# A new order string for visits and jobs in a fused attention and feed-forward kernel

## The chip, the cores and the metric

The kernel runs on one core of one Trainium2 chip. The metric is device time in microseconds, from the start to the end of one execution; a comparison goes by the median of several executions.

## What is computed

One input `x` of 2048 rows and 640 columns is normalised row by row. Attention with 32 query heads of width 20 and a single key and value head shared by all of them, and a feed-forward block with a SiLU between its two matrices, both read the normalised rows, and their results are added to `x`. All arrays are bfloat16. Cut to what matters:

```python
x = A_x                                   # (1, 2048, 640)
xn = layernorm(x)
q = (xn @ wq) -> 32 heads of 20;  k = xn @ wk;  v = xn @ wv      # one k, v head
p = softmax(q @ k.T / sqrt(20));  o = p @ v;  A = concat(o) @ wo
B = silu(xn @ w1) @ w2                    # 640 -> 1728 -> 640
out = x + A + B
```

## The kernel before

The program is written by a planner. Python code creates every operation with its engine, an assumed duration and the keys that it reads and writes; a list scheduler runs a clock over five engines (`pe`, `act`, `dve`, `pool`, `sp`) and fixes the order of the operations on each of them; `emit` then writes each engine's list out, with a semaphore wait wherever an operation depends on another engine. So the order of work on the chip is fixed when the program is built, and the engines then run freely against each other's semaphores.

The scores are cut into blocks: 128 keys by 512 queries of one head. There are 32 heads x 4 query chunks x 16 key tiles = 2048 blocks, ordered in groups of 64 (four heads of one chunk). On PE the work after the prologue falls into three kinds of steps:

- A *visit* (`do_S`, matmuls at line 1133) computes the scores of one to four blocks, each into a PSUM bank of its own. Seven of the eight banks serve visits and jobs. Of a visit's blocks some go to ACT, which takes the exponential of up to three neighbouring banks with one instruction (line 1156, into tile `E`); where the free banks don't lie side by side, the exponential is split into several instructions. The others go to DVE, which builds an exponential from integer arithmetic: line 1173 converts and clamps the block into `Z`, and when three such blocks are together (or the group ends) `flush_z` makes two shifted copies of them, called Y. The second copy is always made by POOL (line 1207), the first by DVE (line 1201) or POOL (line 1207).
- A *P step* (`do_pv`, line 1047) multiplies four blocks of exponentials, one for each head of the group, with the values, in four column strips of the array at once. It accumulates in the eighth bank, which DVE copies out at the group's end (line 1251); a DMA transposes that, and DVE and POOL normalise it.
- A *J step* is one accumulation step of a job: a part of the query projection (`qd_job`), the first feed-forward matrix (`h_job`, 512 columns; its tanh on ACT is line 1395, its product on DVE line 1403) or the output (`out_job`, 320 columns). All of these are four matmuls at line 533 side by side, except the paired step at line 1385. Jobs come in a fixed order from a queue.

The order of the steps on PE is a string, `ORDER`, followed by `follow` from block 70 to the last: P is a P step, J a J step, and every other letter a visit. `VISITS` says what a letter means: its blocks, and how many of them go to DVE. The letter's case is handed on as `y0_on`: a capital sends the first Y copy to DVE, a small letter to POOL, if this visit happens to complete a set.

```python
VISITS = {"a": (3, 0), "b": (3, 1), "c": (3, 2), "e": (4, 1), "f": (4, 2), "g": (2, 0), "h": (2, 1),
          "k": (1, 0), "m": (1, 1), "d": (4, 3)}
```

When a step's inputs or banks aren't there yet by the planner's clock, the planner lets PE wait, or puts a short multiplication by zeros (`fill`, lines 954 and 967) in between. If a P step can't be taken, another may be taken early when a visit needs room, and the string then skips one. Which banks a visit gets, the places in `E`, and the order of the lists of ACT, DVE, POOL and SP all follow from the planner's clock as it goes along the string. After the string's end a tail finishes the last group and the output.

Of the kernel before, what the change touches and what calls it, by code (L numbers as in the profile page):

```python
# [79 lines left out]
YIELD = 0.65  # L80
VISITS = {"a": (3, 0), "b": (3, 1), "c": (3, 2), "e": (4, 1), "f": (4, 2), "g": (2, 0), "h": (2, 1), "k": (1, 0), "m": (1, 1), "d": (4, 3)}
ORDER = (
    "hhPbhPPPhHPbPPPfAPPPPCPBPPbPPFPPgHPPPhBJPJBJPcJJPhGPPPAJJPJCJJPbGPPPHhJPJHhJhhPgJPHhJGPHPGPPPFPPBPPb"
    "PmbPJJaJPcJJPPEPPPPHHHAPPMCPPgPPfJgJJJJGPbJJPPHhJHgPJJhgJPPPBJJbPPbJPBJPBPPPPFPPPAPPfPPJJbJJJPbbPPJJ"
    "JbJJbPPPFPPbJJJbJPJPEJJJJJPPeJJJJJPbhJJJJJPePPPPbPPfPPJJJBhPPJJPEJJJJPJHBJJJPJJPbGJJPPJPfPJPJbJJPPbJ"
    "PJbPJBJJJJbJJJbJPJbJJJbJJPbPPFPPPBPPFPPBPJJJbJJPJBPBJPJJbPJJJbJPJbPPfPPbPPPePJPJbJJBPJbJPJJbPJBJJJJB"
    "JJPbJJJJbPPFPPBPPbPPPEJJJJJJJBPPbJJJBJJJPbJPbPPPfPPbPPBPPePJJJbJPJBPPBJJPbJJJBJPJbJJJJbJJJbPPePPPPFP"
    "PBPPFPPAJJJJJJBPJJJBPJJbJJJbPPEPPPhhPPPfPPBJJJbJJBJJJPaJJbJPJJJPJbJJJbPJPbPPFPPBPPPePPPPFPPbPJPJPgFJ"
    "JJJJJJbJPbPPJbJJJbPPfPPPbPePJJJbJJPBJJBJPJJFPGPPPPbPPfPPJJJBHJJJJJJJePPPPPbcJJJJJBHJJJJJPePPPPbPPfPP"
    "PbJJbJJJbPJJPbJJJBPPbJJJJJBJhJJJJPePPPPBPPfPPBJJJJJbbPPPPPFPPbJJbJJBJPbJJJBJJbPPPPEPPPBPPJJfJJJPJJGb"  # L90
    "PJJJPfPPBPPBJJbPJJJPbBPPPPPBJJJJBJJJbJJJJbJJJJbJJJJbPFPPPPBfPPPPfPPbPPAPJbJJJPeJPPPbPPFPPBJJJJJBJJBJ"
    "JPJbJJPbPJJbJJJBJJPPBPEPPPPPFPPbPJPJbJJPbJJPbJJPbJJJBPPbJJJJBJJPBPPbJJPBPPPEPPbPPJJfJJGPJPFPPBPPBJJJ"
    "JbJJJbJJJJbJJJBJPJbJPJBPPbJPPbPPePPbJJPJJJEJPJJJJJHbPJPBJJPJBJJbPPJJbPPfPPBPPPePPPPFPPbPPJBJJbJJbPPP"
    "FPPBPJJJBJJBJJJJJJJeJPJJJJbJJPBPPEPPPPPdGPPPbPPbJPPBJJJbJJPBJJPBPPbJJJJbJJPBPJbJJJJbPPfPPBPPePJJJJJb"
    "JJJBJJJbJJJPbPJBPPPBJJJJbPPEPPPPFPPbPPPbPPfPPbJJJJJbbPPPJJJbJJbJJJJJPbPPbJPPbJJBJJbPPJJBJJJbPPPPfPPB"
    "PJJCJJJPePPPPaPPBJJJPfJJPPPbhJJJJJPFJJJJJPeJJJJJPBbPPPPJbJPbJJbPJBPPPFPPbPPbJJbJJJBPJJJbJJbJJJPBJJPB"
    "PPFPPBJJJJJBbPPPJJPbJJJbPPPbPPPBPPEPJJJbJJbPPPfPPBPPBJJJJBJJPbPJbJJPBJJJJBJJJJBPPbPJJbPPFPPAPPPfPPJJ"
    "JbJJJBJPJBJJJJbJJJbJJJJBPPePPBJPJJEJJPPBPPbPPPfPPbPPPFPPbPPBPPEPJJJJJBJPJJBJJJBJJJJBJJJJbPPfPPbPPPeP"
    "JJJJJbJJPBJJJBJJPBPPBJPJBJJJJBJPPbPPfPPPBPPePPPPFPPbJPJBJPbJJbPPPfPPBJJJJbJJPJJJJfGJJJJJJPJbJJPbPPfP"
    "PBPPPFPPbPPbPJJBJPJBJJPBPJJBJJJBJPJBPPBJJPBJPJbJPJBPPBPPEJJPJJJbJJPJbJPJBJPbJJJJBJPJbJJPBPPFPPbPPBPP"  # L100
    "PeJPJJJJbJJJBJPJbJJPBJJJbJJJJbPPBPPfPPPbPPePPJJBJJJPEPJJJhJJPePPPPPBPFPPJJbJJPJBPbPJJJcJJPHgJJPJJJGf"
    "PPPPPPbPPfPPBJJPBJPJJbHJJJJJEJJPJJJhbJJJJJPbPPPPePCPJJJJJbbPPPPPPfPPBJJJbPJbPJbJPJJCJJPBPGJJJJJPfGPP"
    "PPPBJJPBJJJJBJJPBJJJbJPPbPJBJJJPbJJJbPPfPPPBPPEPJJJJJbJJJbJJJJBJJJBJJJJbPPFPPAPPPfPPPPFPPBJJJPBJJJJB"
    "JJPaJJJJJJBJJJJPbPEPPPPfPPPPfPPBPPbPPFPPBJJJJBJJJBJPJJbPJJBJPbJPPbJPJBJJJBPPePJJPJJbJJPBPJJbJJJbJPJB"
    "PJJBJJPbJPJBPPFPPgPPEPPPPFPPPbPPFPPBJJJJbJJJBPJJbPJJPBbPJPJJeJJJPJJBPPfPPBPPFPPAPBPJJJJJJfJJJJJGbJJP"
    "JPeJJPJJPJfPbPPPFPPBPPePPbPJJJJEJJPPJJbJJPBJJJBPJbJPbJPJbPJJbPPBPPFPPBPPbPbPFPPbPBPPBPPFPbPPAPPPfbPb"
    "PPFaPPFPPbPPbPePPBPPPKbPJJJJJJBPJJBPPPePA"
)
Z_COST = 0.2
U_PRIO = 1.022  # L110
# [1891 lines left out]
```

## Time and profile before

| | |
|---|---|
| median of 3 runs | 680.25 us (680.22 to 682.18) |
| the profiled execution | 681.0 us, its span 679.1 us |
| granted TensorE clock | 0.999 |
| busy: PE, ACT, DVE, POOL | 668.2, 660.6, 619.7, 573.2 us |
| instructions | 22628 |

The span runs from the first to the last instruction; the execution's own time has 1.9 us more around it. PE is TensorE's matmuls, PEld its weight loads, DVE the vector engine, ACT the scalar engine, POOL GpSimd, SP the queue that issues DMAs. A line of a group reads: source line, engine, operation, output<-input, shapes, xcount | busy us, mean ns of one | idle us just before, and what ended it. A line of the timeline reads: start, length, engine, line, operation, shapes, xcount, and in brackets the idle time before it. Consecutive alike instructions are merged into one line there.

### The profile page before, as it was taken

To read this page: it belongs to the slowest core of one execution; us is meant where nothing else is said; L and a number is where in the kernel's file an instruction comes from. 1 tells how busy PE (TensorE), PEld (TensorE's weight loads), DVE (VectorE), ACT (ScalarE), POOL (GpSimd) and SP (SyncE) were. 2 spreads that over 40 slices of the span, in tenths; PEclk is the share of its full clock that TensorE was granted. 3 is DMA by queue.
4 is the path that set the end of the run, shared out by engine and by line. 5 is a ranking of instruction groups with operands and counts; after the bars stand their busy time and mean duration, and the time that the engine had idled before them with its cause. 6 is when DMAs were issued, how large, how long until landed. Compare 5 with 4: busy or idle time off the path is not lost.

```text
span 679.1 us, 22628 instructions
## 1 busy us (share of the span) xinstructions
PE 668.2 (98%) x9679; PEld 232.9 (34%) x9679; DVE 619.7 (91%) x1086; ACT 660.6 (97%) x774; POOL 573.2 (84%) x472
## 2 busy tenths in 40 slices
PE   9999999999999999999999999999999999999997
PEld 4433333333333333333333323333333333333323
DVE  8799988999999999998999999899989998998995
ACT  6999999999999999999999999999999999999995
POOL 6688799889889998888889787988888989878873
PEclk9999999999999999999999999999999999999999
DMA  7459100000002000101103010100002200000012
GB/s 207 87 197 294 47 16 15 10 13 15 18 17 57 9 19 9 38 14 32 37 10 66 5 20 24 30 16 27 20 23 63 15 9 13 11 19 19 19 25 57
DMA packets 51897, 27.85 MB, mean 41 GB/s; under 512 B 37750, under 2 KB 51158, under 8 KB 51798
## 3 DMA queue, kind: packets, MB, share of 16 engines
q1 hardware_dynamic: 51510, 26.07, 15.2%
q8 instruction: 78, 1.28, 0.8%
q10 hardware_dynamic: 288, 0.33, 0.1%
q14 instruction: 21, 0.17, 0.1%
HBM read 11.44 MB, written 2.62 MB: 21 GB/s over the span
## 4 chain that ended last, share of the span: by engine, by line
PE 71%; ACT 27%; DVE 1%; issue 0%; ACTq 0%
ACT sbt L1156 27%; PE psall L1047 24%; PE psall L533 22%; PE psall L1133 22%; PE psall L967 1%; ACT sbt L1395 1%; DVE sbt L1173 1%; PE psall L1893 1%; PE psall L1385 0%; PE psall L1297 0%; PE psall L1874 0%; PE psall L954 0%; DVE sbt L1403 0%; PE psall L1317 0%; ACT sbt L1742 0%
## 5 line engine op out<-in xcount | busy, mean ns | idle before, releaser
L1156 ACT ACTIVATE sbt<-psall 128x1024 bf16<-128x1024 f32 (+2 forms) x695 | 629.1, 1052 | 3.8 <-PE psall L1133 3.2
L1207 POOL TENSOR_TENSOR sbt<-sbt 128x768 int32<-128x768 int32 (+2 forms) x382 | 532.1, 1421 | 80.3 <-DVE sbt L1201 69.8
L1173 DVE TENSOR_SCALAR sbt<-psall 128x512 int16<-128x512 f32 x707 | 465.6, 686 | 41.3 <-PE psall L1133 32.0
L1047 PE MATMUL psall<-sbt 128*32 128x512 bf16 x3462 | 283.2, 383 | 0.0
L1133 PE MATMUL psall<-sbt 32*128 32x512 bf16 x2048 | 251.7, 384 | 4.1 <-ACT sbt L1156 2.4
L533 PE MATMUL psall<-sbt 128*32 128x320 bf16 (+1 forms) x3863 | 234.7, 331 | 0.1
L1133 PEld LDWEIGHTS psall<-sbt 32*128 32x128 bf16 x2048 | 66.7, 91 | 235.3 <-issue 87.2
L533 PEld LDWEIGHTS psall<-sbt 128*32 128x32 bf16 x3863 | 85.8, 95 | 87.9 <-issue 47.9
L1047 PEld LDWEIGHTS psall<-sbt 128*32 128x32 bf16 x3462 | 72.6, 95 | 100.8 <-issue 68.4
L1201 DVE TENSOR_SCALAR sbt<-sbt 128x1536 int16<-128x1536 int16 (+1 forms) x106 | 60.3, 578 | 0.5
L1403 DVE SCALAR_TENSOR_TENSOR sbt<-sbt,psall 128x512 bf16<-128x512 bf16 (+1 forms) x56 | 38.0, 679 | 1.3 <-ACT sbt L1395 1.2
L1395 ACT ACTIVATE sbt<-psall 128x512 bf16<-128x512 f32 x54 | 34.6, 641 | 0.5 <-PE psall L533 0.2
L1239 POOL TENSOR_TENSOR sbt<-sbt 128x320 bf16<-128x320 bf16 x31 | 22.6, 729 | 4.3 <-DVE sbt L1201 4.2
L1251 DVE CAST sbt<-psall 128x512 bf16<-128x512 f32 x31 | 21.2, 684 | 1.2 <-PE psall L1047 0.8
L967 PE MATMUL psall<-sbt 128*128 128x512 bf16 (+5 forms) x53 | 14.9, 422 | 1.8 <-DVE sbt L1656 1.2
L1501 DVE SCALAR_TENSOR_TENSOR sbt<-psall,sbt 128x320 bf16<-128x320 f32 x28 | 13.4, 487 | 1.8 <-PE psall L533 1.5
L1722 DVE BATCH_NORM_STATS2 sbt<-sbt 128x6 f32<-128x320 bf16 x26 | 11.3, 466 | 2.6 <-DMA sbt<-in_A_x_dram 2.6
L1352 DVE TENSOR_SCALAR sbt<-psall 128x512 bf16<-128x512 f32 (+1 forms) x19 | 13.0, 684 | 0.3
L1748 POOL TENSOR_SCALAR sbt<-sbt 128x640 bf16<-128x640 bf16 x8 | 7.0, 878 | 5.5 <-DVE sbt L1790 2.6
L967 PEld LDWEIGHTS psall<-sbt 128*128 128x128 bf16 x53 | 5.2, 108 | 8.5 <-issue 3.8
L954 PE MATMUL psall<-sbt 128*32 128x512 bf16 (+10 forms) x25 | 7.8, 333 | 0.0
L1234 DVE RECIPROCAL sbt<-sbt 128x16 f32<-128x16 bf16 x31 | 7.6, 244 | 0.0
(87 smaller groups left out, 87.1 us busy)
## 6 DMA issues: line engine op xcount, KB each, us to landing
sbt<-in_A_x_dram SPq DMA_DIRECT2D x31, 160.0 KB, 3.6
out_dram<-sbt SPq DMA_DIRECT2D x15, 160.0 KB, 1.8
sbt<-in_B_w_dram SPq DMA_DIRECT2D x5, 432.0 KB, 5.8
sbt<-sbt SPq DMA_DIRECT2D x105, 20.0 KB
sbt<-in_B_w_dram SPq DMA_DIRECT2D x13, 160.0 KB, 2.9
sbt<-sbt SPq DMA_DIRECT2D x1, 1024.0 KB, 6.0
sbt<-sbt SPq DMA_TRANSPOSE x56, 2.4
sbt<-in_A_wo_dram SPq DMA_DIRECT2D x5, 160.0 KB, 2.8
```

The lines of the kernel that those rows point to most:

```text
L533: ins = pe.matmul(self.bk(b, 0, n, j, j + SLOT), w[:, j:j + SLOT], x, start=start, stop=stop, tile_position=(0, j), skip_group_check=True)
L967: return pe.matmul(self.bk(b, 0, n), self.zero[:, 0:P], self.zero[:, 0:n], start=True, stop=True)
L1047: ins = pe.matmul(self.bk(UBANK, 0, QW, r, r + SLOT), self.v[:, it.w, it.kt, :], it.x(), start=f, stop=False, tile_position=(0, r), skip_g ...
L1133: ins = pe.matmul(self.bk(bank[i]), self.kT[r:r + SLOT, 1 if i in dv else 0, kt * P:(kt + 1) * P], self.qT[r:r + SLOT, g % 8, (g // 8) % 2 ...
L1156: return a.activation(self.E[:, (b0 + lo) * QW:(b0 + lo + m) * QW], self.ps[:, b * BANK:(b + m) * BANK], AF.Exp, scale=ACT_SCALE)
L1173: return v.tensor_scalar(self.Z[:, zs, zp * QW:(zp + 1) * QW], self.bk(bb), 0.0, ZMAX, ALU.max, ALU.min)
L1201: sc.new("dve", td, lambda v, k=k: v.tensor_scalar(self.Y[:, zs, k, 0:w], self.Z[:, zs, 0:w], float(PH[k + 1][0]), None, ALU.add), zk, yk, ...
L1207: sc.new("pool", tp, lambda v, k=k, cb=cb: v.tensor_tensor(self.Y[:, zs, k, 0:w].bitcast(I32), self.Z[:, zs, 0:w].bitcast(I32), cb, ALU.ad ...
L1239: op = sc.new(eng, 0.75 if eng == "pool" else t_dve_ps(16 * DH), lambda v: v.tensor_tensor(dst, ut[:, :, :, 0:DH], rb, ALU.mult), [key, (" ...
L1251: ev = sc.new("dve", t_dve_ps(QW), lambda v: v.tensor_copy(self.U[:, up, :], self.bk(UBANK)), [("UB",)], [("U", up)], prio=U_PRIO, name=f" ...
L1395: sc.new("act", t_act(QW), lambda a: a.activation(t, src, AF.Tanh, scale=0.5), [("B", b)], [("tb", tp)], prio=X_PRIO, name=f"th{c}_{fk}")
L1403: sc.new("dve", t_dve_ps(QW), lambda v, r0=r0, r1=r1, ht=ht: v.scalar_tensor_tensor(out=ht[r0:r1, :], in0=t[r0:r1, :], scalar=1.0, in1=src ...
```

## The change

Only the string `ORDER` is replaced by another of the same length, 2441 letters. Nothing else differs.

```diff
 YIELD = 0.65
 VISITS = {"a": (3, 0), "b": (3, 1), "c": (3, 2), "e": (4, 1), "f": (4, 2), "g": (2, 0), "h": (2, 1), "k": (1, 0), "m": (1, 1), "d": (4, 3)}
 ORDER = (
-    "hhPbhPPPhHPbPPPfAPPPPCPBPPbPPFPPgHPPPhBJPJBJPcJJPhGPPPAJJPJCJJPbGPPPHhJPJHhJhhPgJPHhJGPHPGPPPFPPBPPb"
-    "PmbPJJaJPcJJPPEPPPPHHHAPPMCPPgPPfJgJJJJGPbJJPPHhJHgPJJhgJPPPBJJbPPbJPBJPBPPPPFPPPAPPfPPJJbJJJPbbPPJJ"
-    "JbJJbPPPFPPbJJJbJPJPEJJJJJPPeJJJJJPbhJJJJJPePPPPbPPfPPJJJBhPPJJPEJJJJPJHBJJJPJJPbGJJPPJPfPJPJbJJPPbJ"
-    "PJbPJBJJJJbJJJbJPJbJJJbJJPbPPFPPPBPPFPPBPJJJbJJPJBPBJPJJbPJJJbJPJbPPfPPbPPPePJPJbJJBPJbJPJJbPJBJJJJB"
-    "JJPbJJJJbPPFPPBPPbPPPEJJJJJJJBPPbJJJBJJJPbJPbPPPfPPbPPBPPePJJJbJPJBPPBJJPbJJJBJPJbJJJJbJJJbPPePPPPFP"
-    "PBPPFPPAJJJJJJBPJJJBPJJbJJJbPPEPPPhhPPPfPPBJJJbJJBJJJPaJJbJPJJJPJbJJJbPJPbPPFPPBPPPePPPPFPPbPJPJPgFJ"
-    "JJJJJJbJPbPPJbJJJbPPfPPPbPePJJJbJJPBJJBJPJJFPGPPPPbPPfPPJJJBHJJJJJJJePPPPPbcJJJJJBHJJJJJPePPPPbPPfPP"
-    "PbJJbJJJbPJJPbJJJBPPbJJJJJBJhJJJJPePPPPBPPfPPBJJJJJbbPPPPPFPPbJJbJJBJPbJJJBJJbPPPPEPPPBPPJJfJJJPJJGb"
-    "PJJJPfPPBPPBJJbPJJJPbBPPPPPBJJJJBJJJbJJJJbJJJJbJJJJbPFPPPPBfPPPPfPPbPPAPJbJJJPeJPPPbPPFPPBJJJJJBJJBJ"
-    "JPJbJJPbPJJbJJJBJJPPBPEPPPPPFPPbPJPJbJJPbJJPbJJPbJJJBPPbJJJJBJJPBPPbJJPBPPPEPPbPPJJfJJGPJPFPPBPPBJJJ"
-    "JbJJJbJJJJbJJJBJPJbJPJBPPbJPPbPPePPbJJPJJJEJPJJJJJHbPJPBJJPJBJJbPPJJbPPfPPBPPPePPPPFPPbPPJBJJbJJbPPP"
-    "FPPBPJJJBJJBJJJJJJJeJPJJJJbJJPBPPEPPPPPdGPPPbPPbJPPBJJJbJJPBJJPBPPbJJJJbJJPBPJbJJJJbPPfPPBPPePJJJJJb"
-    "JJJBJJJbJJJPbPJBPPPBJJJJbPPEPPPPFPPbPPPbPPfPPbJJJJJbbPPPJJJbJJbJJJJJPbPPbJPPbJJBJJbPPJJBJJJbPPPPfPPB"
-    "PJJCJJJPePPPPaPPBJJJPfJJPPPbhJJJJJPFJJJJJPeJJJJJPBbPPPPJbJPbJJbPJBPPPFPPbPPbJJbJJJBPJJJbJJbJJJPBJJPB"
-    "PPFPPBJJJJJBbPPPJJPbJJJbPPPbPPPBPPEPJJJbJJbPPPfPPBPPBJJJJBJJPbPJbJJPBJJJJBJJJJBPPbPJJbPPFPPAPPPfPPJJ"
-    "JbJJJBJPJBJJJJbJJJbJJJJBPPePPBJPJJEJJPPBPPbPPPfPPbPPPFPPbPPBPPEPJJJJJBJPJJBJJJBJJJJBJJJJbPPfPPbPPPeP"
-    "JJJJJbJJPBJJJBJJPBPPBJPJBJJJJBJPPbPPfPPPBPPePPPPFPPbJPJBJPbJJbPPPfPPBJJJJbJJPJJJJfGJJJJJJPJbJJPbPPfP"
-    "PBPPPFPPbPPbPJJBJPJBJJPBPJJBJJJBJPJBPPBJJPBJPJbJPJBPPBPPEJJPJJJbJJPJbJPJBJPbJJJJBJPJbJJPBPPFPPbPPBPP"
-    "PeJPJJJJbJJJBJPJbJJPBJJJbJJJJbPPBPPfPPPbPPePPJJBJJJPEPJJJhJJPePPPPPBPFPPJJbJJPJBPbPJJJcJJPHgJJPJJJGf"
-    "PPPPPPbPPfPPBJJPBJPJJbHJJJJJEJJPJJJhbJJJJJPbPPPPePCPJJJJJbbPPPPPPfPPBJJJbPJbPJbJPJJCJJPBPGJJJJJPfGPP"
-    "PPPBJJPBJJJJBJJPBJJJbJPPbPJBJJJPbJJJbPPfPPPBPPEPJJJJJbJJJbJJJJBJJJBJJJJbPPFPPAPPPfPPPPFPPBJJJPBJJJJB"
-    "JJPaJJJJJJBJJJJPbPEPPPPfPPPPfPPBPPbPPFPPBJJJJBJJJBJPJJbPJJBJPbJPPbJPJBJJJBPPePJJPJJbJJPBPJJbJJJbJPJB"
-    "PJJBJJPbJPJBPPFPPgPPEPPPPFPPPbPPFPPBJJJJbJJJBPJJbPJJPBbPJPJJeJJJPJJBPPfPPBPPFPPAPBPJJJJJJfJJJJJGbJJP"
-    "JPeJJPJJPJfPbPPPFPPBPPePPbPJJJJEJJPPJJbJJPBJJJBPJbJPbJPJbPJJbPPBPPFPPBPPbPbPFPPbPBPPBPPFPbPPAPPPfbPb"
-    "PPFaPPFPPbPPbPePPBPPPKbPJJJJJJBPJJBPPPePA"
+    "hhPhbPPPCkPbPPPfAPPPPCPbPPbPPfPPaMPPPHBJPJBPJcJJPhgPPPAJJPJCJJPbgPPPHhJJPHhJHhPgJPHHJgPHPgPPPfPPBPPb"
+    "mPbPPJAJPcJJJPEPPPPHhHaPPmCPPGPPFJJGJJJGPbJJPJckJHGPPJhgJPJPbJJbPPBPPbJPBPPPPfPPPAPPfPPJJBJPbJPJbJPJ"
+    "JBJJPbPPfPPbJJJbPJJPfJJJPJJPePJJJJJBhJJJJJPePPPPBPPfJJJJJBgJPJPPPfJJPJPhBJJJPJJbGPJJPJJfPPPJbPJJJPBP"
+    "PJbJPBJJJJbJJJbPJJBJJJBJPJbPPFPPPBPPFPPBJPJJBJPPJBJBJPJJJBJJJBPPJbPPfPPbPPPePJPJBJJbJPBJJPJbJJJbJPJb"
+    "JJJJbJPJBPPFPPBPPBPPPEJJJJJJJbJJPBPJBJPJJbPJBPPPfPPBPPbPPePJJJbJJPbPPBJPJbJJJBPJJbJJJJBJJJbPPePPPPFP"
+    "PBPPfPPAPJPBJJJJJJbJJJJBJJJBPPEPPPmbPPPfPPbJJJbJJBJPJJbJPAPJJJJJJBPPBJJJJbPPfPPBPPPePPPPFPPBJPPJGPFJ"
+    "JPJJJbPJBJJJJBJPJbPPFPPbPPEPJJJbJJPBJJBPJJJFPPGPPPFPPbPPJJJbhJJJJJJJePPPPPBcJJJJJEmJJJJJPePPPPBPPFPP"
+    "PBJJBJJJbPJJPBJJBPPJbJJJJJbJJJJJHePPPPPbPPFPPBPJJbJJJbPPPPFPPBJJJbPbJJPBJJBJJJbPPPPePPBJPPJfJJJPPBGJ"
+    "JJJJPfPPBPPBJJbJPJJPBBPPPPPBJJJJBJJJbJJJJbJJJBJJJJJbPFPPPPFPbPPPBPPfPPAPJBJJPJePPJPbPPFPPbPJJJbJJPBJ"
+    "JPBJPBJJJJBJJJbJJJJaPPfPPPPPFPPBPJJJbJPJBJPJbJJJBPJPbPPJBJJBJPPBPJJBJJPbPPEPPPBPJPJfJJPgJPfPPBPPbPJJ"
+    "bJJJJBJJJBJJJJBPJJBPJBPJJbPJPbPPEPPBPJJJJJEJJJJJJPCGPJPBPPJBJJJJBPJJbPPFPPBPPPEPPPPFPPbPJJBJPbJJbPPP"
+    "FPPBJJJJPbJbJJJJJJJeJPJJJJbJJPbPPEPPPPPdGPPPBPPbJJPBJJPbJPJBJPJBPJJbJJJbPJJBPJJbJJPbPPfPPBPPePJJJJJb"
+    "JJJBJJJBJJPPBJJBPPPBJJJJbPPePPPPfPPbPPPBPPfPPbJJJJJbBPPPJJJbJJBJPJJbPJJbJPPJBPJbJJbPPJJJbJJBPPPPfPPP"
+    "BJJCJJJPEPPPPAPPBJPJJfJPJPPbhJJJJJPfJJJJJPEJJJJJPBbPPPPJbPJBJJbPJBPPPFPPBPPBJJbJJJbJPJJBJJbJJPJBJJPB"
+    "PPFPPbJJJJJbbPPPJPJBJJJBPbPPPPPbPPePJJJbJJBPPPFPPBPPBPJJBJJPBPJJBJJJJbJJJBPJJbJJPbJPJbPPfPPaPPPfPPJJ"
+    "JBJPJbJJJBJJJJbJJJBJJJJBPPePPBPJJJEJJPPBPPbPPPfPPBPPPFPPBPPbPPEPJJJJJbJJJJBJJJPbJJJbJJJJbPPfPPBPPPEP"
+    "JJJJJBJJJBPJJBJPPbPJBPJJBJJJJJbPPbPPfPPPBPPePPPPFPPbPJJbPJbJJbPPPFPPBJJJJbPJJJJJJfgJPJJJJJJBJPJBPPfP"
+    "PbPPPFPPbPPbJPPBJJJbJJPBJJJbPJJBJPJBJPJbPPbJPJbPJJbPPBPPEJJPJJJbJJJPbJJJBJPJbJPJbPJJbJJPbPPfPPBPPBPP"
+    "PEPJJJJJbJPJbJPBJJJJbJJJBJJJJbPPFPPbPPPbPPePPJJbJJJPePJJJHJJPePPPPBPPFPJJJBJBJPPbJPJPCJJJJgHJJJPJPGf"
+    "PPPPPbPPPfPPbJJPbPJJJbhJJJJJeJJJJJPhbJJJJJPbPPPbPPfPJJJJJbBPPPPPPfPPbJJPBJJbPJBPJJJCJJPAJJJHJJPPGfPP"
+    "PPPbJJJJBJJJbJPJbJJJJBPPbJJJBJPPBJPJbPPfPPBPPPePJJJJJbJJJBJJJJBJJJbJJJJBPPFPPAPPPfPPPPFPPbPJJJBJJBJJ"
+    "JJPaJJJbJJJJJJJPBPEPPPPfPPPPfPPBPPbPPFPPBJJPJbJJJbJJPBJPJbJJJbJPPBPJBJJJJBPPEPPBJJJJJJJBJPJBJJPBPPBJ"
+    "JJJBJPJbJPJBPPFPPAPPBPPPPFPPPbPPFPPBJJPBJJBJJJJbJJJPbPbJPPJJeJJJPJJbPPfPPBPPBPPePPBJJJJJJJeJJJJJJBJP"
+    "PJJEhPJJJPFPbPPPFPPBPPEPBJPPJJEPJPJJJBJJJbJJPBPJJBPJBJPPbPJbJPJBPPFPPBbPPBPPFPPbPPBPPBBPPFPAPPPPfBPB"
+    "PPFPAPPFPPPPBBPEPBPPPkBPJJJJJJBJJPBPPEPPA"
 )
 Z_COST = 0.2
 U_PRIO = 1.022
```

## The prediction

> **What bounds the kernel now.** I read the page first, then the groups of instructions with shapes kept apart, then the timeline of single visits, then the waits, and last the busy time of three stretches. The page:
>
> ```profile
> span 679.1 us, 22628 instructions
> PE 668.2 (98%) x9679; PEld 232.9 (34%) x9679; DVE 619.7 (91%) x1086; ACT 660.6 (97%) x774; POOL 573.2 (84%) x472
> PE 71%; ACT 27%; DVE 1%; issue 0%; ACTq 0%
> ```
>
> PE and ACT are both busy nearly all the time, and the chain that ended last passes from one to the other. A busy share does not say how far each is from its own limit, since neighbouring instructions overlap. The timeline of a few visits gives the prices of PE's slots (four matmuls, one token of the string):
>
> ```profile
> 302.06 0.39 PE L1133 MATMUL psall<-sbt 32*128 32x512 bf16 x3
> 302.38 0.61 PE L1047 MATMUL psall<-sbt 128*32 128x512 bf16 x8
> 302.93 0.39 PE L1133 MATMUL psall<-sbt 32*128 32x512 bf16 x3
> 303.25 0.73 PE L533 MATMUL psall<-sbt 128*32 128x320 bf16 x16
> 303.91 0.39 PE L1133 MATMUL psall<-sbt 32*128 32x512 bf16 x3
> 266.95 1.05 PE L1047 MATMUL psall<-sbt 128*32 128x512 bf16 x16
> 337.85 8.35 ACT L1156 ACTIVATE sbt<-psall 128x1024 bf16<-128x1024 f32 x9
> ```
>
> Four P slots take 1.05 us and two take 0.61, so a P is (1.05 - 0.61) / 2, about 0.22; against 302.38 to 302.93 I use 0.216. A visit starts 0.32 us before the slot after it, 0.105 more than a slot, and the same 0.105 is lost going back (0.55 for two P). So every unbroken stretch of visits costs 0.21 us beside its slots. Four J of 320 columns take 0.66 - 0.105, so 0.137 each (rounded down). On ACT, nine two-bank exponentials in a row take 8.35 us; less the last one's own 1.08 (next fence) that is 0.91 from start to start.
>
> ```profile
> L1156 ACT ACTIVATE sbt<-psall 128x1024 bf16<-128x1024 f32 x560 | 535.7, 1082 | 2.8 <-PE psall L1133 2.3
> L1156 ACT ACTIVATE sbt<-psall 128x1536 bf16<-128x1536 f32 x43 | 63.1, 1486 | 1.0 <-PE psall L1133 0.9
> L1156 ACT ACTIVATE sbt<-psall 128x512 bf16<-128x512 f32 x92 | 55.9, 668 | 0.0
> L1395 ACT ACTIVATE sbt<-psall 128x512 bf16<-128x512 f32 x54 | 34.6, 641 | 0.5 <-PE psall L533 0.2
> L1133 PE MATMUL psall<-sbt 32*128 32x512 bf16 x2048 | 251.7, 384 | 4.1 <-ACT sbt L1156 2.4
> L533 PE MATMUL psall<-sbt 128*32 128x320 bf16 x2448 | 128.9, 302 | 0.1
> L533 PE MATMUL psall<-sbt 128*32 128x512 bf16 x1415 | 105.7, 382 | 0.0
> ```
>
> A bank more costs ACT 0.414 us (1082 - 668 ns), so one, two and three banks and a tanh are taken at 0.496, 0.91, 1.324 and 0.496. The order string can now be laid along the trace: its visits cover 1978 blocks, all but the first 70 of the 2048 L1133 matmuls, in order, so each visit has a start time. The string's 936 J are 360 of 512 columns and 576 of 320, by the matmuls that stand between the visits.
>
> ```profile
> 42.78 0.69 PE L1133 MATMUL psall<-sbt 32*128 32x512 bf16 x4 [0.30 <-ACT sbt L1156]
> 667.16 0.39 PE L1133 MATMUL psall<-sbt 32*128 32x512 bf16 x3
> 42.80:137.90 95.10, 94.04 (x1231) 30.64 (x1231) 88.20 (x150) 94.27 (x126) 83.89 (x62) 1.00 0.25 74
> 137.90:615.70 477.80, 476.81 (x7201) 161.80 (x7197) 445.10 (x743) 475.49 (x540) 415.77 (x314) 1.00 0.10 23
> 615.70:667.20 51.50, 49.80 (x695) 16.73 (x693) 46.20 (x80) 51.30 (x60) 43.23 (x33) 1.00 0.12 26
> ```
>
> First to last visit is 624.4 us. The string's slots and stretches add up to 604.0 us on PE and, with the tanhs, 609.4 on ACT: two engines, both full. Taken in twelve pieces of about 53 visits, with the larger of the two sums in each, the floor is 612.8: 93.1 of the first 95.1 us, 469.1 of the middle 477.8 (PE decides, by up to 0.7 us a piece, in all but one), 50.6 of the last 51.5 (ACT decides; PE has 44.9). So order alone can win at most 11.6 us, about 1 us in each piece; the work itself is there in any order.
>
> **The change, part by part.** Only the string differs. Counting tokens: 636 visits, 1978 blocks, 869 P and 936 J in both, and P and J stay at their places to within a few tokens all along the string. Of the 636 gaps before visits 220 have other P and J in them, 49 visits are of another kind, and 232 differ in case alone.
>
> *PE.* Unbroken stretches of visits go from 584 to 586: 2 x 0.21 = +0.42 us, on the path, since PE decides the middle. P and J may alternate as they like: 303.25 to 303.91 shows nothing lost inside a stretch of them, and a P beside a J has the same 0.216.
>
> *ACT.* Exponentials by banks: two-bank 517 in both, three-bank 67 to 68, one-bank 50 to 46. That is 1.324 - 4 x 0.496 = -0.66 us; with the mean durations, latency included, 1.486 - 4 x 0.668 = -1.19. The starts decide throughput: -0.66, less than half of it where ACT decides. Where a visit finds no neighbouring banks its exponential is split, at 2 x 0.496 - 0.91 = 0.08 us: the trace has 92 one-bank instructions where the string and the first 70 blocks ask for little over 50. Ten splits more or fewer are +-0.8 us; I take zero. The Trainium skill ("ScalarE: Activation LUTs", section "What ACT_TABLE_LOAD costs") gives an ACTIVATE with immediate operands 186 ns + 0.833 ns an element and an overlap of 93 ns back to back, an estimate of 0.946 us for two banks. By that the string's ACT work would be some 635 us, more than the 624.4 it ran in, so the row's 0.91 stands; the change's ACT term would be -0.71 by the page.
>
> *DVE and POOL.*
>
> ```profile
> L1207 POOL TENSOR_TENSOR sbt<-sbt 128x768 int32<-128x768 int32 x354 | 510.1, 1467 | 77.2 <-DVE sbt L1201 67.1 <-DVE sbt L1173 9.8
> L1173 DVE TENSOR_SCALAR sbt<-psall 128x512 int16<-128x512 f32 x707 | 465.6, 686 | 41.3 <-PE psall L1133 32.0
> L1201 DVE TENSOR_SCALAR sbt<-sbt 128x1536 int16<-128x1536 int16 x98 | 57.1, 590 | 0.4
> POOL sbt L1207 <- DVE sbt L1201: 69.8, 87, 1.9
> PEld psall L1047 <- POOL sbt L1207: 6.6, 28, 0.4
> ```
>
> A capital matters only where a visit completes a set of three Z blocks: then the set's first copy goes to DVE (0.59 us) and not to POOL (1.467). Capitals rise from 292 to 330, yet counting the sets by the planner's rule gives 105 on DVE before (the trace has 106 in all) and 108 after; 32 sets change engine, nearly as many each way. DVE gets 3 x 0.59 and one block (0.686): +2.5 us of its 619.7; POOL loses 3 x 1.467 = 4.4. Each set on DVE keeps POOL waiting 0.80 us (69.8 / 87), so POOL nets -2.0. The Trainium skill ("SBUF — State Buffer", section "Who interferes with whom") has one of the two engines blocked for the whole of the other's instruction; by that a moved set holds POOL only 0.59, and POOL nets -2.6. Neither engine is at the end of the chain (DVE 1%), and 41.3 us of waiting ahead of L1173 are DVE's cover. If that cover is gone, the whole 2.5 us would be paid; I take 0.
>
> *Stalls.* The sums hardly move: the floor counted anew in the same twelve pieces is 613.3, +0.5. What is left is how much of the 11.6 us changes, and no row prices that. The lower bound takes it all (-11.6), the upper is open: one wait at a place like this one costs
>
> ```profile
> 267.93 0.39 PE L1133 MATMUL psall<-sbt 32*128 32x512 bf16 x3
> 268.50 0.40 PE L1133 MATMUL psall<-sbt 32*128 32x512 bf16 x4 [0.18 <-DVE sbt L1173]
> 268.37 1.94 ACT L1156 ACTIVATE sbt<-psall 128x1024 bf16<-128x1024 f32 x2 [0.19 <-PE psall L1133]
> ```
>
> Two visits back to back here (tokens "Bf") needed all seven banks: the second came 0.57 us after the first instead of 0.216, and ACT stood 0.19 us without work. The new string has "F", a P, "b", three P, "B" around this place: the pair is gone. Back-to-back pairs that ask for seven banks fall from 3 to 1. More widely, 49 visits start over 0.15 us later than their slots explain; 28 of these are visits whose own gap or kind is rewritten, 57%, against 39% (249 of 636) of all visits. So the edits lean towards places that lose time, but only lean: most of the stall is spread in bits of 0.03 to 0.15 us, and the spread of the gaps around ACT's need is 0.31 us before and after. In the last piece it grows (visits in pairs where P and visit alternated evenly). I take 15% of the slack recovered, -1.7 us: the excess of 18 points at the long stalls, scaled down for those that reappear.
>
> Sum: +0.4 PE, ACT and DVE 0, stalls -1.7: -1.3 us. The profiled execution took 681.0 us (span 679.1), the median of the runs shown is 680.25; so 679.7 for such an execution and 679.0 for the median.
>
> **The rivals.**
> *Faster by more.* The edits removed the long stalls and made no new ones: a third of the slack goes, -3.9 + 0.4, about 676.8. For it: the lean above, and the pairs gone. Against: PE's stretches are no fewer, and ACT's gaps no evener.
> *Slower, by ACT running dry.* ACT is full to within 15 us in 624, so each new gap that is too long for the one or two exponentials queued costs what the place above shows, 0.19 us, and nothing pays it back. It decides from 11 new such moments (11 x 0.19 = 2.1 us); one in ten of the 220 rewritten gaps is 22, 4.2 us: 684.4. The place is the middle, where both sums lie within 1 us, and the last piece with its new pairs. For it: 220 places, and a reserve of only 2%. Against: the totals stay aligned all along, so a long gap has a short one beside it.
> *Slower, by DVE.* The 2.5 us more are paid in full: 682.7. Against: the rows above give it 41 us of cover.
> *Nothing happens.* Most of the rewriting has no effect (200 of the 232 case flips; P and J exchanged inside a gap), the rest cancels: 680.3, inside my forecast's case.
>
> **How the numbers follow.** Under 0.3% (2.0 us) cannot be told from no change. The forecast's case, with "nothing happens" in it, 0.42, reaching from 678.2 to 682.2; faster 0.32; ACT dry 0.20 and DVE 0.06, together 0.26 slower. The range from 675.6 to 683.6 leaves out the worse half of the dry case and the best end of the faster one.
>
> **What would show it.** Right: L1156 with two-bank, three-bank and one-bank counts near 560, 44 and 88; L1201 x109 and L1207 near 379; the window sums of first, middle and last stretch each within 1 us of now; the stall at "Bf" gone. Wrong: ACT's idle before its two-bank exponentials well over the 2.8 us of now, or many more than 92 one-bank exponentials (ACT dry or split), or DVE's 41.3 us of waiting before L1173 mostly gone (DVE the bound).

## The result, and the profile after

The changed kernel takes 680.0 us in the median (678.99 to 681.34, 19 runs) against 680.76 us before (680.22 to 682.73, 19 runs): a ratio of 0.9984, with a 95% interval of 0.9977 to 0.9992. It is faster by 0.16%. The interval leaves out 1, but the step is smaller than the 0.3% that the prediction set as the bound of what can be told. The forecast was 679.0 / 680.25 = 0.9982.

The page of the changed kernel, its first lines and the chain that ended last:

```profile
span 679.2 us, 22635 instructions
PE 669.3 (99%) x9681; PEld 232.9 (34%) x9684; DVE 621.9 (92%) x1090; ACT 659.6 (97%) x768; POOL 569.2 (84%) x469
PE 85%; ACT 14%; DVE 0%; issue 0%; ACTq 0%
```

Nothing seems to have happened: the span is 679.2 us and was 679.1. In this execution the gain is hidden by a loss ahead of the string. The busy time in stretches of 2 us of the changed kernel (columns: stretch, its length, busy us of PE, PEld, DVE, ACT and POOL, granted clock, DMA share, GB/s):

```profile
20.00:22.00 2.00, 0.99 (x14) 0.54 (x12) 1.97 (x8) 2.00 (x3) 1.12 (x2) 1.00 0.36 82
22.00:24.00 2.00, 1.36 (x24) 1.03 (x24) 1.70 (x10) 1.88 (x3) 0.24 (x1) 0.91 0.36 82
24.00:26.00 2.00, 2.00 (x14) 1.18 (x13) 0.80 (x3) 0.61 (x1) 0.64 (x1) 0.50 0.06 14
```

The clock goes to half in the prologue, which the change does not touch: for 3.41 us by the profile's clock record, from 23.64 to 27.05. So the string's first visit comes at 44.77 us and not at 42.78, 1.99 us later. The last visit comes 0.65 us later (667.81 against 667.16), and the end of the span 0.07; behind the last visit lie 11.37 us and not 11.95. From the first visit on the two traces can be laid beside each other, at visits where both strings have used up the same blocks, P and J. The table is worked out from the starts of the L1133 matmuls: us gained (-) or lost since the first visit, against the kernel before. The kernels of the experiments stand below.

| at (us, before) | 127.7 | 239.0 | 272.5 | 327.1 | 463.5 | 619.8 | 641.4 | 667.2 |
|---|---|---|---|---|---|---|---|---|
| changed kernel | -0.38 | -0.52 | -0.60 | -0.79 | -0.84 | -0.86 | -1.25 | -1.34 |
| e1_skeleton | -0.31 | -0.44 | -0.30 | -0.33 | -0.38 | +0.12 | -0.26 | +0.65 |
| e1_case | -0.07 | +0.59 | +0.68 | +0.90 | +1.07 | +2.20 | +2.20 | +2.19 |
| e1_unselected | +3.53 | +5.79 | +6.56 | +7.15 | +11.65 | +15.64 | +15.91 | +16.35 |
| e1_new_to_1763 | -0.38 | -0.52 | -0.59 | -0.78 | -0.83 | -0.77 | -0.78 | -0.78 |
| e2_old_to_1763 | -0.06 | -0.07 | -0.07 | -0.07 | -0.07 | -0.14 | -0.53 | -0.62 |
| e2_letter | -0.38 | -0.52 | -0.60 | +1.96 | +2.34 | +2.37 | +2.56 | +4.96 |
| e3_late_copy | -0.37 | -0.51 | -0.59 | +0.50 | +0.45 | +0.44 | +0.05 | -0.04 |
| e2_warm | -0.38 | -0.53 | -0.61 | -0.80 | -0.86 | -0.87 | -1.26 | -1.35 |

Two executions of the new string agree to 0.02 us in it (the rows of the changed kernel and of e2_warm). With the old string they agree less well: e2_old_to_1763 has the lists of before up to 604 us, and is 0.07 us ahead of it by 82 us, where e1_case is ahead as much. So the one profiled execution of before lost 0.07 us there by itself, and the rows of the table, which are taken against it, hold that. Steps of a tenth of a microsecond can still be read, which no median shows. The string brings -1.34 us, or -1.27 without that place, in small steps: -0.41 by 137 us, about -0.4 from there to 327, next to nothing for 300 us, and -0.5 in the last stretch.

### The profile page after: what moved, and what is told of

It reads as the page before. It is cut to its first block, busy times and chain, and to the rows that moved or that the text cites. A ratio compares the mean times of both kernels' runs of the same rounds, so it can differ in the third digit from the quotient of the medians.

```text
span 679.2 us, 22635 instructions
## 1 busy us (share of the span) xinstructions
PE 669.3 (99%) x9681; PEld 232.9 (34%) x9684; DVE 621.9 (92%) x1090; ACT 659.6 (97%) x768; POOL 569.2 (84%) x469
## 3 DMA queue, kind: packets, MB, share of 16 engines
HBM read 11.44 MB, written 2.62 MB: 21 GB/s over the span
## 4 chain that ended last, share of the span: by engine, by line
PE 85%; ACT 14%; DVE 0%; issue 0%; ACTq 0%
PE psall L1047 29%; PE psall L1133 26%; PE psall L533 26%; ACT sbt L1156 14%; PE psall L967 2%; PE psall L1893 1%; PE psall L1385 0%; PE psall L954 0%; ACT sbt L1395 0%; PE psall L1874 0%; DVE sbt L1173 0%; PE psall L1317 0%; DVE sbt L1403 0%; PE psall L1297 0%; ACT sbt L1742 0%
## 5 line engine op out<-in xcount | busy, mean ns | idle before, releaser
L1207 POOL TENSOR_TENSOR sbt<-sbt 128x768 int32<-128x768 int32 (+2 forms) x379 | 528.1, 1421 | 82.5 <-DVE sbt L1201 73.0
L1173 DVE TENSOR_SCALAR sbt<-psall 128x512 int16<-128x512 f32 x708 | 465.4, 684 | 38.1 <-PE psall L1133 28.5
L1133 PE MATMUL psall<-sbt 32*128 32x512 bf16 x2048 | 251.7, 384 | 3.5 <-ACT sbt L1156 2.1
L533 PE MATMUL psall<-sbt 128*32 128x320 bf16 (+1 forms) x3863 | 237.7, 331 | 0.2
L1133 PEld LDWEIGHTS psall<-sbt 32*128 32x128 bf16 x2048 | 66.0, 91 | 234.2 <-issue 84.5
L533 PEld LDWEIGHTS psall<-sbt 128*32 128x32 bf16 x3863 | 87.9, 95 | 86.9 <-issue 45.3
L1047 PEld LDWEIGHTS psall<-sbt 128*32 128x32 bf16 x3464 | 72.9, 95 | 102.2 <-issue 69.3
L1201 DVE TENSOR_SCALAR sbt<-sbt 128x1536 int16<-128x1536 int16 (+1 forms) x109 | 62.5, 581 | 0.6
L954 PE MATMUL psall<-sbt 128*32 128x512 bf16 (+8 forms) x27 | 7.7, 320 | 0.0
```

The costliest lines, as they stand in the source:

```text
L533: ins = pe.matmul(self.bk(b, 0, n, j, j + SLOT), w[:, j:j + SLOT], x, start=start, stop=stop, tile_position=(0, j), skip_group_check=True)
L1047: ins = pe.matmul(self.bk(UBANK, 0, QW, r, r + SLOT), self.v[:, it.w, it.kt, :], it.x(), start=f, stop=False, tile_position=(0, r), skip_g ...
L1133: ins = pe.matmul(self.bk(bank[i]), self.kT[r:r + SLOT, 1 if i in dv else 0, kt * P:(kt + 1) * P], self.qT[r:r + SLOT, g % 8, (g // 8) % 2 ...
L1173: return v.tensor_scalar(self.Z[:, zs, zp * QW:(zp + 1) * QW], self.bk(bb), 0.0, ZMAX, ALU.max, ALU.min)
L1201: sc.new("dve", td, lambda v, k=k: v.tensor_scalar(self.Y[:, zs, k, 0:w], self.Z[:, zs, 0:w], float(PH[k + 1][0]), None, ALU.add), zk, yk, ...
L1207: sc.new("pool", tp, lambda v, k=k, cb=cb: v.tensor_tensor(self.Y[:, zs, k, 0:w].bitcast(I32), self.Z[:, zs, 0:w].bitcast(I32), cb, ALU.ad ...
```

## The experiments

My theory was that the gain is order: fewer waits where steps that stood badly next to each other were moved. The rivals were the choice of engine for the Y copies (the case of the letters), letters and case fitted to each other, and an order that hardly matters.

**e1_skeleton**: the new string's letters in the old string's case.

```diff
 (the first seven visits of the string; the fifth and the sixth differ)
-    "hhPhbPPPCkPb...
+    "hhPhbPPPcKPb...   # every visit's case as in the old string
```

> The new string's letters and places with the old string's case, visit by visit. My theory (the gain is order: which steps stand next to each other at places that stalled): -1.0 to -1.3 us against before, like the full change. Rival 1 (the gain is the choice of engine for the Y copies): 0 to -0.3 us. Rival 2 (letters and case are fitted to each other, each Y copy timed against DVE's neighbouring work): slower than before by 1 to 3 us, since 32 sets go to the other engine than the places were chosen for.

682.4 us (681.32 to 683.8, 12 runs) against 681.2 before (29 runs): 1.0013 [1.0001, 1.0024]. Slower than either kernel, at the lower end of rival 2's expectation (+1.2 us by the medians, +1.1 by the runs at full clock, 681.75 against 680.62). My theory asked for -1.0 to -1.3 and failed. Up to 239 us this kernel keeps nearly all of the gain (-0.44 of -0.52); then it loses at single places, +0.43 at the visit of 288 us (most of which comes back by 295) and 0.9 us after 655.

**e1_case**: the old string's letters in the new string's case.

```diff
 (later in the string)
-    "...JbJPJJbPJBJJJJBJJPb...
+    "...JBJPJJbPJbJJJJbJJPb...   # every visit's case as in the new string
```

> The old string's letters and places with the new string's case, visit by visit; 108 sets on DVE. My theory (order alone): within 0.5 us of before. Rival 1 (engine of the Y copies): -1.0 to -1.3 us. Rival 2 (fitted to each other): slower than before by 1 to 3 us.

682.49 us (682.19 to 684.18, 12 runs) against 681.2: 1.0020 [1.0010, 1.0029], which is +1.3 us by the medians, +1.8 by the runs at full clock (682.46 against 680.62) and +2.2 by the visits. Again rival 2, and again not my theory, which allowed 0.5 us. Neither half of the change is worth anything alone over the whole string. Up to 239 us the order brings the gain even with the old case; behind that it does so only with the case that was chosen for it.

**e1_unselected**: as many rewritten gaps as in the change, but made by chance.

```diff
-    "hhPbhPPPhHPbPPPfAPPPPCPBPPbPPFPP...
+    "hhPbhPPPhHPbPPPfAPPPPCPPBPbPPFPP...   # 220 gaps, by random exchanges of neighbours
```

> The old string after random exchanges of neighbouring letters (P, J or visit), unselected, until 220 gaps before visits differ, as many as in the change; counts of every letter as before. If any rewriting of 220 gaps is nearly free because ACT's and DVE's queues even it out: within 2 us of before. By the dry-ACT price of the prediction (0.19 us in one gap of ten): +4 us. If the order is worth more than that because PE, ACT and DVE wait in turn: +10 to +20 us, with ACT's idle and one-bank exponentials both up.

697.5 us (696.24 to 698.35, 4 runs) against 681.2: 1.0235 [1.0216, 1.0254], 16 us, in the upper of the three expectations. The groups of that kernel:

```profile
L1156 ACT ACTIVATE sbt<-psall 128x1024 bf16<-128x1024 f32 x553 | 531.4, 1049 | 10.1 <-PE psall L1133 6.8
L1156 ACT ACTIVATE sbt<-psall 128x512 bf16<-128x512 f32 x100 | 57.6, 643 | 0.3 <-PE psall L1133 0.3
L1173 DVE TENSOR_SCALAR sbt<-psall 128x512 int16<-128x512 f32 x707 | 465.3, 686 | 52.4 <-PE psall L1133 45.0
```

The same work as before, and ACT's idle time ahead of its two-bank exponentials rises from 2.8 to 10.1 us, DVE's ahead of L1173 from 41.3 to 52.4, most of both until PE has written the scores. PE does not run ahead either: from the first visit to the last it has 81 matmuls of `fill` and not 23, so the planner itself saw PE short of work. One unselected rewritten gap costs 16 / 220 = 0.07 us, and the loss grows all along the string, though not evenly (table). The change's 220 gaps cost less than nothing, so they were hardly drawn by chance. I take it that they were chosen so that PE, ACT and DVE still fit each other; this is one random string that moves no visit to another kind, and it does not show by what the change was chosen.

**e1_new_to_1763** and **e2_old_to_1763**: the two strings spliced where their counts of blocks, P and J agree.

```diff
-ORDER = ( ...the old string... )   # in effect; the kernels hold the spliced string itself
+ORDER = NEW[:2211] + OLD[2211:]     # e1_new_to_1763
+ORDER = OLD[:2211] + NEW[2211:]     # e2_old_to_1763
```

> The new string up to block 1763 + 70, from there on the old one (the two stand at the same count of blocks, P and J there). The traces of before and after put -0.75 us before this point and -0.6 us behind it. If a local saving stays where it is made and is carried to the end: -0.7 us against before. If the last stretch is limited by ACT anyway and takes the saving back: 0. If it is the whole that is fitted: slower than before.

> The old string up to block 1763 + 70, from there on the new one: the other half of the splice. If local savings add up (-0.75 before this point, -0.6 behind it): visits to this point as in before to 0.1 us, then -0.5 to -0.6 at the last visit, so -0.6 us against before. If they don't add up: 0, or slower.

680.1 us against 681.2 (12 and 29 runs), 0.9983 [0.9974, 0.9993]; and 681.02 against 680.93 (12 and 22 runs), 0.9995 [0.9985, 1.0005], which by the median alone cannot be told from no change. By the visits they are -0.78 and -0.62 us, together -1.40. The 0.07 us that the execution of before lost by itself is in both; counted once, they make -1.33 against the -1.34 of the whole. Local savings add up, and a saving made at 128 us is still there at 667.

**e2_letter**: the changed kernel with one letter's case turned.

```diff
-    "JPBJPBJJJJBJJJbJJJJaPPfP...
+    "JPbJPBJJJJBJJJbJJJJaPPfP...   # the visit at 281 us, which completes a set
```

> The changed kernel with the case of a single letter turned (a B at about 281 us becomes b, so that one set of three Z blocks is copied by POOL in 1.47 us instead of by DVE in 0.59). If a set's engine is work moved between two engines with cover, as the prediction priced it: within 0.3 us of the changed kernel, so -0.8 to -1.3 us against before. If letters and case are fitted to each other: up to 1 us lost near 281 us, nothing after. If the late copy makes the planner wait and sends everything behind it into other banks and another fit: +3 to +8 us, lost step by step after 281 us.

686.56 us (685.37 to 687.1, 6 runs) against 680.93: 1.0075 [1.0058, 1.0091], some 6 us above the changed kernel (685.4 against 679.2 by the runs at full clock), for one copy moved from DVE to POOL. Against the changed kernel the visits lose 6.3 us, in steps: 2.8 us by 327 us (1.1 of it at one visit, 295.5), and 2.5 in the last 26 us of the string, some 360 us after the letter.

**e3_late_copy**: the same letter turned and the same copy moved, but the planner is told that POOL needs no time for it, so that PE's, ACT's and SP's lists are held.

```diff
 (cut to the planner's part; LETTER = 812 picks this one set)
-            sc.new("pool", tp, lambda v, k=k, cb=cb: v.tensor_tensor(
+            sc.new("pool", 0.0 if self.b_next == LETTER and k == 0 else tp, lambda v, k=k, cb=cb: v.tensor_tensor(
```

> The same set as in e2_letter is copied by POOL and not by DVE, but the planner is told that POOL needs no time for it: PE's, ACT's and SP's lists stay exactly those of the changed kernel, and only this copy moves from DVE's list to POOL's. Turning the letter lost 6 us in the run e2_letter. If that came from the late copy itself, by engines waiting for it and for each other: +4 to +7 us again against the changed kernel. If it came from the planner's new lists behind the letter, which bring fills, other banks and another order: at most the 0.9 us by which POOL's copy is longer, lost near 281 us and nowhere else, so 0 to +0.9 us against the changed kernel.

680.74 us (680.46 to 682.62, 11 runs) against 681.09: 0.9998 [0.9987, 1.0009]. The timeline of PE, first of this kernel and then of the changed one, at the place:

```profile
286.07 1.08 PE L1047 MATMUL psall<-sbt 128*32 128x512 bf16 x16
288.17 0.40 PE L1047 MATMUL psall<-sbt 128*32 128x512 bf16 x4 [1.02 <-POOL sbt L1207]
288.50 0.40 PE L1133 MATMUL psall<-sbt 32*128 32x512 bf16 x4
```

```profile
285.98 1.26 PE L1047 MATMUL psall<-sbt 128*32 128x512 bf16 x20
287.17 0.39 PE L1133 MATMUL psall<-sbt 32*128 32x512 bf16 x4
287.50 0.61 PE L1047 MATMUL psall<-sbt 128*32 128x512 bf16 x8
```

The fifth of five P steps needs the late copy and waits 1.02 us for POOL. The visit behind it comes 1.24 us later than in the changed kernel, and from 292 us on the trace keeps 1.29 to 1.30 us, to the last visit. I had allowed 0.9; POOL has no gap at this place, it makes six copies in a row there (8.58 us from 280.96). So a late copy has no cover here, and it costs once what it costs. The other 5 us of e2_letter come with the planner's new lists: from the string's start on, PE's steps are in the same order in e3_late_copy as in the changed kernel and in another at many places of e2_letter, which has 51 matmuls of `fill` between its first and last visit, and not 26. Which of these places costs how much was not tested.

**e2_warm** and **e3_warm_old**: three multiplications by zeros in the prologue where PE stands nearly idle, with the new and with the old string.

```diff
+            if n0 == 4:
+                def warm(pe, b):
+                    return pe.matmul(self.bk(b, P, BANK), self.zero[:, 0:P], self.zero[:, 0:BANK - P], start=True, stop=True)
+                mms[0:0] = [(0.0, warm)] * 3
```

> The changed kernel with three multiplications by zeros (384 columns) ahead of the second v job in the prologue, into columns of its own bank that nobody reads; the planner is told that they take no time, so all else is in the same order. In the profile of the changed kernel the granted clock is 0.50 from 24 to 26 us, just after PE had stood idle or at 20-column matmuls for most of 21.2 to 23.6 us; 8 of its 19 runs have a mean clock of 0.997, the others 0.999 or 1.0 and some 1.7 us less. If those idle us are what lowers the clock: no run at 0.997, median about 679.2, ratio to before about 0.9975. If the lowered window comes whatever PE does there: 4 of 10 runs at 0.997 and a median near 680.0. If the multiplications are themselves in the way: 0.2 to 0.5 us later in every run.

> The kernel before with the three multiplications by zeros of e2_warm in its prologue. If the lowered clock is the prologue's matter and no part of the change: all runs at a clock of 0.999 or 1.0, median about 680.6, ratio to before about 0.9990, and 1.3 us above e2_warm, which is the change's own worth without the clock. If the change altered how often it comes: no gain here.

With the new string: 679.19 us (678.9 to 679.75, 10 runs) against 680.93, 0.9967 [0.9956, 0.9978], and no run under a mean clock of 0.999. Its median lies below those of both kernels. In the same set of runs, 19 of the 40 of kernels without the multiplications (before, e2_letter, e2_old_to_1763) had a mean clock of 0.998 or less. The profile by itself proves nothing, since the clock can stay without the multiplications too. First two stretches of e1_new_to_1763, which has the prologue of the changed kernel, then one of e2_warm:

```profile
22.00:24.00 2.00, 1.38 (x29) 1.21 (x26) 1.43 (x8) 1.87 (x3) 0.74 (x1) 1.00 0.29 65
24.00:26.00 2.00, 2.00 (x27) 0.64 (x24) 1.70 (x5) 1.31 (x2) 0.33 (x2) 1.00 0.35 81
22.00:24.00 2.00, 1.89 (x32) 1.52 (x31) 1.41 (x9) 1.85 (x3) 0.65 (x1) 1.00 0.34 77
```

PE is busy 1.89 of the 2 us from 22 to 24 in e2_warm. It was 1.36 in the changed kernel, where the clock fell, and 1.38 in e1_new_to_1763, where it stayed; the last section says what differs. With the old string the multiplications gave 680.62 us against 681.09, 0.9991 [0.9982, 1.0000]. The median is the expected one, but not for the expected reason: 3 of 11 runs still had a mean clock of 0.997, against 5 of 21 at 0.997 or less before, so a rarer window isn't shown here, and the runs at full clock alone differ nearly as much (680.45 against 680.86), which stays unexplained. The profiled run is one of the three, and there the lowered window lies later, where the string begins:

```profile
44.00:46.00 2.00, 1.94 (x25) 0.48 (x21) 1.96 (x4) 2.00 (x4) 2.00 (x2) 0.73 0.11 25
46.00:48.00 2.00, 2.00 (x18) 0.43 (x16) 1.37 (x3) 1.52 (x4) 2.00 (x3) 0.50 0.10 25
```

So in the new string's runs the weak place in the prologue seems mended, and with the old string a second one showed. Whether the new string is safe at the second place, or ten runs merely missed it, stays open.

## Why the prediction was right, point by point

*The size.* -1.3 us was forecast (+0.4 for PE, -1.7 from stalls); the string itself brought -1.27 to -1.34. Runs at full clock say the same: 679.22 us (11 runs) against 680.47 to 680.86 before (13 to 17 runs in each of the experiments' sets), and within one set 679.19 of e2_warm against 680.47. The median is 680.0 and not 679.0 because 8 of the 19 runs had the lowered clock, 1.75 us each (680.98 against 679.22), which the prediction did not know of: the profile of before had no such window.

*PE and ACT.* The groups of the changed kernel (the last two lines with all shapes together):

```profile
L1156 ACT ACTIVATE sbt<-psall 128x1024 bf16<-128x1024 f32 x563 | 539.0, 1082 | 2.4 <-PE psall L1133 1.7
L1156 ACT ACTIVATE sbt<-psall 128x1536 bf16<-128x1536 f32 x44 | 64.9, 1497 | 2.6 <-PE psall L1133 2.5
L1156 ACT ACTIVATE sbt<-psall 128x512 bf16<-128x512 f32 x82 | 50.6, 676 | 0.0
L1173 DVE TENSOR_SCALAR sbt<-psall 128x512 int16<-128x512 f32 x708 | 465.4, 684 | 38.1 <-PE psall L1133 28.5
L1207 POOL TENSOR_TENSOR sbt<-sbt 128x768 int32<-128x768 int32 (+2 forms) x379 | 528.1, 1421 | 82.5 <-DVE sbt L1201 73.0
L1201 DVE TENSOR_SCALAR sbt<-sbt 128x1536 int16<-128x1536 int16 (+1 forms) x109 | 62.5, 581 | 0.6
```

563, 44 and 82 exponentials were read where 560, 44 and 88 were named: three splits fewer than I took, within the bound given for them. The three stretches took what they took before to within 1 us, and PE stayed on the chain throughout, more than before (85% against 71%).

*Stalls.* By the prediction's slot prices, the time by which visits start later than their slots explain (over 0.03 us each) went from 22.1 to 20.4 us: -1.7, the term itself. That is no second measurement: it is what those prices leave of the -1.34 once +0.4 is taken off. How it came about was only half as argued. At the 28 rewritten of the 49 long stalls, 7.2 us became 3.8; at the 21 others 6.2 became 5.4; and 3.3 us of long stalls appeared elsewhere. These parts depend on which visit of one string is set beside which of the other (visit by visit in order, they are about 6.9 to 2.3, 6.7 to 7.0, and 3.6 elsewhere), their sum does not: -0.9. The lean towards stalling places was real, and the new stalls gave some three quarters of it back. The other -0.8 came from stalls under 0.15 us, for which the prediction named no place. That it left 15% was my choice and not derived: that the size came out is luck. The place shown, "Bf" at 268 us, is a case of it: the pair is gone and 0.14 us with it, and a short fill that the planner put in at 273.6 us (trace of the changed kernel) gave back the same 0.14. The largest single step is at 627.6 us (before), 0.24 us. First two lines of before, then one of the changed kernel:

```profile
627.38 0.33 PE L954 MATMUL psall<-sbt 128*32 128x384 bf16 x1
628.08 1.02 ACT L1156 ACTIVATE sbt<-psall 128x1024 bf16<-128x1024 f32 x1 [0.19 <-PE psall L1133]
626.06 3.96 ACT L1156 ACTIVATE sbt<-psall 128x1024 bf16<-128x1024 f32 x5
```

Before, a visit `e` is followed by five J, two P and a fill, and ACT stands 0.19 us without work until the next visit. The new string has visits `E` and `h` side by side and three J and two P behind them; the fill is gone from this gap and ACT's exponentials run on. A fill in the next gap takes 0.07 us of it back.

*The last stretch.* I named its new pairs of visits as a place where ACT could run dry. It gained 0.5 us instead, as in the lines above.

*DVE and POOL.* Priced at nothing, and in the sum that held: L1201 and L1207 came out at 109 and 379 instructions, as counted, and DVE's wait before L1173 went only from 41.3 to 38.1 us. But the reason given was wrong, and that the term came out at nothing is luck too. Idle time of DVE and POOL is no cover for a copy that a P step needs soon: e3_late_copy shows 1.24 us for one copy, and e1_case shows that the case alone, put on the old string, costs 1.8 us at full clock, where I had priced it at nothing. The 32 sets that change engine were part of the change's worth.

*The rivals.* "Slower, by ACT running dry" was priced at 0.19 us in one gap of ten, 4.2 us. Unselected edits of that number cost 16, with ACT's idle time ahead of its two-bank exponentials up by 7.3 and DVE's ahead of L1173 by 11.1: ACT does run dry there, though not it alone, and 4.2 us was a quarter of what such edits cost. In the change it did not happen (2.4 us of that idle time, 2.8 before). That the edits were selected is the likely reason, not a shown one; the profile had a faint sign of it, the lean of 57% against 39%. "Faster by more" fell short, as far as the count above tells, because PE's long stalls came back elsewhere.

## What to carry to other kernels

When two engines are each full to within 2 to 3%, add up what the order cannot change before judging a new order; what is left (here 11.6 of 680 us, by the slot prices) is all that it can win, while an unselected order can lose more (here 16). Compare traces at places where both programs have done the same work: steps of 0.1 us show there that no median resolves. Where lists are planned ahead, one late operation can cost little as long as the lists stay (1.3 us here); planning around it can cost several times as much (6.3).

## What the runs showed of the hardware

The granted clock dropped to half for 3.41 us in some executions only, and each time cost 1.1 to 2.0 us (medians of runs with and without it, kernel by kernel): in the prologue, where PE was idle or at 20-column matmuls for most of the 2.4 us before, or at the start of the string. The same program at the same place kept its clock in the others. The Trainium skill ("TensorE: Matmul & The Clock Gate", section "What's actually happening") gives windows of 3413 ns that run on regardless of the program, and that agrees: 3.41 us in all four records of a lowered clock, and a start that does not follow the program's own time.

This can be read from the clock records of the eleven profiles. Full clock begins 3.98 to 6.73 us after the first instruction, and every later change comes a whole number of 3.413 us behind that: five in the changed kernel (6.57 and 23.64 us), in e1_skeleton and in e3_late_copy, twelve in e3_warm_old. So each execution has a grid of such windows, and what differs is how the grid lies on the program. In those first three a window began at 20.1 to 20.4 us, PE was busy for 55 to 64% of it, and the next one was at half clock. In the six other profiles without the three multiplications, the grid cut the same place into two windows, with PE busy 70 to 76% and 82 to 86%, and the clock stayed. The profile of e2_warm has its grid near theirs, so it would probably have kept its clock in any case, and only the ten runs speak for the multiplications. Busy time is not all that counts: in e3_warm_old the window ahead of the lowered one had 90%, and a window of 70% at 286.6 us in e3_late_copy was followed by full clock. What is counted stays open.

Unexpected too was how exactly such a program can repeat. Visits of two executions of the new string agree to 0.03 us over 620 us, apart from the lowered window; with the old string the execution of before differed by 0.07 us at one place, and that of e3_warm_old, behind its lowered window, by 0.16 us at another (319 us). More differs behind the last visit: the old string's end took 11.95, 11.44 and 11.13 us to the end of the span (before, e3_warm_old, e1_new_to_1763).
